# Bias table of a fused attention and expert kernel: two scalings and one hidden unit on ScalarE, sixteen transfers on GpSimd's queue

## The chip, the cores and the metric

The kernel runs on one core of a Trainium2 chip. The metric is the device time of one execution in microseconds (us), the median of three runs. The core has a matrix engine (TensorE, PE in the profile), three engines for elementwise work (VectorE is DVE, ScalarE is ACT, GpSimd is POOL) and SyncE (SP), which here only issues DMA transfers. ScalarE and GpSimd can issue transfers too.

## The reference

Attention over 8 batches, 8 heads, 576 queries and keys of 64 numbers, with a learned bias that depends on the distance of query and key, then a layer of 8 experts of which each token takes one:

```python
scores = scale * np.matmul(q, k.transpose(0, 1, 3, 2))
psi_rel = np.log1p(np.abs(rel))                       # rel = i - j
psi_i = np.log1p(np.maximum(pos[:, None], 1.0))
x = (psi_rel / psi_i)[..., None]
bias = np.maximum(x @ w1 + b1, 0.0) @ w2              # 32 hidden units, 8 heads
scores = scores + bias.transpose(2, 0, 1)[None, :, :, :]
...                                                   # softmax, times v
h = np.maximum(x[mask] @ w1[e], 0.0)                  # the expert of each token
out[mask] = gate_w[mask, None] * (h @ w2[e])
```

The bias is the same for all batches, so the kernel computes it once, ahead of the attention, as a table for 576 queries, 8 heads and 576 keys.

## The kernel before

**Stages.** First the bias table (from about 6 us to about 60 us), then attention over 32 pairs of heads (to about 555 us), then the expert layer. The order of the instructions on each engine is the order in which the Python program names them (a manual schedule). The framework adds the waits between engines.

**One block of the table.** `bias_table` (L225) goes through 32 blocks of 16 queries in the order of `SEQ`. For each block four "hidden units" of 128 rows and 576 columns are made (`bias_hidden`, L180: add a shift, then the maximum with 0). By L232 the first of the four goes to ScalarE and three to VectorE; blocks listed in `ON_DVE` have all four on VectorE. The first unit is made ahead: at each step L239 asks for those of this and the next block. TensorE multiplies each unit with the second weights (`bias_out`, L194) into a PSUM bank, of which there are three. One step later (`LAG = 1`) `bias_put` (L208) scales the bank by a number for each query, into one of eight buffers that are used in turn (`bias_outs`, L176). The scaling is ScalarE's, but VectorE's for the blocks in `PUT_DVE`.

**Where the table goes.** SP issues one transfer of 288 KB for each of the 32 blocks, to `NBm` (L218), which serves queries 0 to 511. The last 64 queries are blocks 32 to 35. They are run in the order 32, 34, 33, 35 by `bias_late` (L255), whose steps the first two units of the attention loop call (`LATE`, L133): 32 and 34 are put in the first unit, 33 and 35 in the second. Each of these blocks is written to `NBr` by four transfers of 72 KB (L223), `par` 0 and 1 times `a` 0 and 1; the two of `par` 0 on SP's queue, the two of `par` 1 on GpSimd's.

**What reads them.** Scores of a pair are made in five units (`scores`, L381): units 0 to 3 read `NBm`, unit 4 reads `NBr`. A VectorE reduction (L409) adds the scores in PSUM and the table, and takes the minimum. The reduction of unit 4 reads rows of all of `NBr`, so it needs all sixteen transfers. It also frees the PSUM bank into which TensorE makes the next pair's first scores (L395).

**What GpSimd and SP do around it.** In the order of its program GpSimd has the transfers of blocks 32 and 34, a copy of unit 0 (`compact`, L429), the transfers of 33 and 35, the copy of unit 1, the low part of pair 1's queries (`split`, L379), the copy of unit 2, the low part of its keys (L379), the copy of unit 3. SP has, behind the eight transfers of L223, the values of pair 0 (L365) and the queries and keys of pair 2 (L350 to L355).

Of the kernel before, what the change touches and what calls it, by code (L numbers as in the profile page):

```python
# [44 lines left out]
GS = 8  # L45
# [63 lines left out]
class Attn:  # L109
# [9 lines left out]


    SEQ = (0, 4, 1, 5, 2, 6, 3, 7, 8, 12, 9, 13, 10, 14, 11, 15, 16, 20, 17, 21, 18, 22, 19, 23, 24, 28, 25, 29, 26, 30, 27, 31)
    ON_DVE = (4,)


    LAG = 1
    PUT_DVE = (22, 31, 33)
    TURN0, SPLIT0, QK1 = (4, 8), (6, 10), (9, 10, 11, 12, 13, 14, 15, 16)
    V0 = (0, 1)
    ROUTE = (6, 7, 8, 15, 16, 18)
# [78 lines left out]
    def bias_put(self, blk, parts):  # L208
        nc = self.nc
        o = next(self.bias_outs)  # L210
        for cols, ps in parts:
            if blk in self.PUT_DVE:
                nc.vector.tensor_scalar_mul(o[:, cols], ps, self.rpsi[:, blk : blk + 1])
            else:
                nc.scalar.activation(o[:, cols], ps, AF.Copy, scale=self.rpsi[:, blk : blk + 1])
        if blk < NMAIN:
            c, k = divmod(blk, GS)
            nc.sync.dma_start(self.NBm[k:P:GS, H * c : H * c + H, :], o)  # L218
        else:
            for par in range(2):  # L220
                for a in range(2):
                    r = 64 * par + 2 * (blk - NMAIN) + a
                    (nc.sync, nc.gpsimd)[par].dma_start(self.NBr[r : 64 * par + 64 : GS, :, :], o[64 * a + par : 64 * a + 64 : 2, :])  # L223

    def bias_table(self, hooks):  # L225

# [3 lines left out]
        def ahead(blk, cg):  # L230
            if blk < NMAIN and (blk, cg) not in ready:
                by = "act" if cg == 0 and blk not in self.ON_DVE else "dve"  # L232
                ready[blk, cg] = self.bias_hidden(blk, cg, by)

        with self.tc.tile_pool(name="bps", bufs=3, space=PSUM) as pp:
            done = []
            for at, blk in enumerate(self.SEQ):
                ps = pp.tile([P, 1024], F32, tag="bps", name=f"bps{blk}")
                for b in self.SEQ[at : at + 2]:  # L239
                    if b not in self.ON_DVE:  # L240
                        ahead(b, 0)
# [1250 lines left out]
```

## Time and profile before

| | |
|---|---|
| median of three runs | 995.18 us (994.75 to 996.34) |
| the profiled execution | 995.04 us, its span 993.2 us |
| TensorE busy | 968.3 us, 97% of the span |
| VectorE, ScalarE, GpSimd busy | 704.7, 710.2, 319.0 us |

The profile is of one execution, in us from the start of its span. An operation is named by its line in the kernel, its engine, and the tiles it writes and reads (`out<-in`). A bracket at the end of a row of the timeline is the time that the engine was idle before it, and what ended that wait. The share of the DMA engines is a mean over 16 of them and can come out a little over 1, since packets overlap.

### The profile page before, as it was taken

The page shows a single profiled execution, that of the slowest core. Times are in us where ns is not written, and L with a number is a line of the kernel's source. Part 1 is how long each engine was busy: PE and PEld are TensorE (multiplying, and loading weights), DVE is VectorE, ACT ScalarE, POOL GpSimd, SP SyncE. Part 2 cuts the span into 40 slices and gives each one's busy share as a digit, 9 for nine tenths or more (in the row PEclk, how much of TensorE's full clock was granted, in tenths as well). Part 3 has the DMA queues.
Part 4 walks back from the last instruction along what each step waited for, and adds up shares of the span by engine and source line. Part 5 has one row for each costly group of instructions (what it writes and reads, how often), then busy time and mean ns, then how long its engine had stood idle before and what let it go on. Part 6 is the DMA issues. An engine that isn't in the chain of part 4 may idle for free.

```text
span 993.2 us, 22468 instructions
## 1 busy us (share of the span) xinstructions
PE 968.3 (97%) x8110; PEld 760.0 (77%) x8110; DVE 704.7 (71%) x1441; ACT 710.2 (72%) x1366; POOL 319.0 (32%) x497
## 2 busy tenths in 40 slices
PE   7989999999999999999999999999999999999996
PEld 4556766767667677776667699989999998989895
DVE  8976677776777777777877677986665665555555
ACT  6989888888888888888888655555545555555554
POOL 1633333635436254362542523511111111111111
PEclk9999999999999999999999999999999999999999
DMA  6997855465554656546469441221118821252510
GB/s 164 191 192 149 214 113 104 102 132 110 131 101 101 133 106 135 101 101 136 94 119 207 136 113 54 81 64 43 44 49 223 248 66 43 87 172 82 175 44 25
DMA packets 327480, 116.34 MB, mean 117 GB/s; under 512 B 283438, under 2 KB 304302, under 8 KB 327362
## 3 DMA queue, kind: packets, MB, share of 16 engines
q1 hardware_dynamic: 320914, 95.21, 43.4%
q0 software_dynamic: 6304, 19.63, 5.9%
q8 instruction: 65, 1.06, 0.5%
q14 instruction: 53, 0.43, 0.2%
q10 hardware_dynamic: 144, 0.00, 0.0%
HBM read 144.34 MB, written 33.34 MB: 179 GB/s over the span
## 4 chain that ended last, share of the span: by engine, by line
PE 78%; DVE 7%; ACT 4%; issue 3%; DMA 1%; SPq 0%; POOL 0%; DVEq 0%; POOLq 0%; ACTq 0%
PE p L1211 19%; PE p L1228 16%; PE sps L395 13%; PE xps L481 13%; PE eps L439 10%; ACT Eb L424 2%; ACT eT L327 2%; PE eps L445 1%; DVE Eb L409 1%; PE xps L467 1%; DVE xTb L329 1%; DVE w1lo L1169 1%; PE xps L753 1%; DVE w2lo L1169 1%; PE xps L784 1%
## 5 line engine op out<-in xcount | busy, mean ns | idle before, releaser
L409 DVE CUSTOM_DVE_ANT_0 Eb<-sps,NBm 128x576 f32<-128x576 f32 x256 | 183.6, 754 | 122.3 <-PE sps L395 49.0
L424 ACT ACTIVATE Eb<-Eb,mn 128x576 f32<-128x576 f32 x288 | 220.9, 769 | 10.5 <-DVE mn L409 9.5
L327 ACT ACTIVATE eT<-eps 128x512 f32<-128x512 f32 x256 | 148.9, 595 | 54.3 <-PE eps L439 53.3
L395 PE MATMUL sps<-QK 64*128 64x288 f32 (+1 forms) x1728 | 170.7, 309 | 4.1 <-DVE mn L409 3.6
L395 PEld LDWEIGHTS sps<-QK 64*128 64x128 f32 (+1 forms) x1728 | 133.4, 185 | 44.6 <-DVE mn L409 25.3
L1211 PE MATMUL p<-QK,w1hi 128*128 128x256 f32 x1136 | 160.9, 284 | 0.1
L439 PE MATMUL eps<-idf,Eb 128*128 128x128 f32 x1024 | 148.8, 279 | 3.7 <-DVE eT L329 1.9
L1211 PEld LDWEIGHTS p<-QK,w1hi 128*128 128x128 f32 x1136 | 147.2, 192 | 3.3 <-issue 1.8
L481 PE MATMUL xps<-eT,vraw 128*64 128x288 f32 x1024 | 149.3, 416 | 0.0
L439 PEld LDWEIGHTS eps<-idf,Eb 128*128 128x128 f32 x1024 | 112.6, 141 | 37.5 <-issue 13.3
L1214 DVE SCALAR_TENSOR_TENSOR hl<-p,hh 128x512 fp32r<-128x512 f32 x72 | 49.7, 691 | 119.0 <-ACT hh L1213 98.2
L1237 POOL DMA_INDIRECT out<-mo,idt x36 | 47.0, 1307 | 256.7 <-ACT mo L1236 169.4
L1213 ACT ACTIVATE hh<-p 128x512 fp32r<-128x512 f32 x72 | 43.1, 598 | 117.9 <-PE p L1211 113.7
L1228 PE MATMUL p<-w2hi,hh 128*128 128x512 f32 x288 | 112.3, 390 | 0.0
L1228 PE MATMUL p<-w2hi,hl 128*128 128x512 f32 x288 | 112.3, 390 | 0.0
L429 POOL COPY rem<-Eb 128x128 f32<-128x128 f32 x128 | 37.2, 292 | 215.9 <-ACT Eb L424 214.8
L1169 DVE TENSOR_TENSOR w2lo<-NBm,w2hi 128x1024 fp32r<-128x1024 f32 x72 | 89.5, 1243 | 16.2 <-ACT w2hi L1168 16.2
L481 PEld LDWEIGHTS xps<-eT,vraw 128*64 128x64 f32 x1024 | 62.3, 136 | 40.0 <-issue 12.6
L1211 PE MATMUL p<-QK,w1lo 128*128 128x256 f32 x568 | 91.3, 283 | 0.0
L1169 DVE TENSOR_TENSOR w1lo<-NBm,w1hi 128x1024 fp32r<-128x1024 f32 x72 | 84.1, 1208 | 0.0
L1211 PEld LDWEIGHTS p<-QK,w1lo 128*128 128x128 f32 x568 | 78.3, 192 | 0.0
L1168 ACT CAST w2hi<-NBm 128x1024 fp32r<-128x1024 f32 x72 | 74.9, 1040 | 0.0
(220 smaller groups left out, 1453.2 us busy)
## 6 DMA issues: line engine op xcount, KB each, us to landing
NBm<-moe_w SPq DMA_DIRECT2D x84, 512.0 KB
NBm<-moe_w SPq DMA_DIRECT2D x42, 1024.0 KB
NBr<-xg SPq DMA_DIRECT2D x80, 128.0 KB
kraw<-k SPq DMA_DIRECT2D x128, 72.0 KB
xd<-xt SPq DMA_DIRECT2D x128, 72.0 KB
vraw<-v SPq DMA_DIRECT2D x64, 128.0 KB
NBm<-xTb SPq DMA_DIRECT2D x24, 288.0 KB
NBm<-moe_w SPq DMA_DIRECT2D x3, 2048.0 KB
```

What stands on the lines that cost most here:

```text
L327: self.nc.scalar.activation(out, ps, AF.Copy, scale=scale)
L395: nc.tensor.matmul(self.sps[h][:, half, 0:HS], QK[o, q, qs], QK[o, k, HS * half : HS * half + HS], start=i == 0, stop=i == 2, skip_group_c ...
L409: nc.vector.tensor_tensor_reduce(out=e.rearrange("p (t w) -> p t w", t=2), in0=self.sps[h][:, :, 0:HS], in1=nb.rearrange("p (t w) -> p t w ...
L424: self.nc.scalar.activation(e, e, AF.Exp, bias=mn, scale=-1.0, accum_out=sm)
L439: nc.tensor.transpose(ps[:, k, :], e[:, part, P * k : P * k + P], self.idf)
L481: nc.tensor.matmul(ps[out : out + 64, :], lhsT, rhs, tile_position=(row, out), skip_group_check=True, **kw)
L1168: self.nc.scalar.copy(h, w)
L1169: self.nc.vector.tensor_tensor(l, w, h.bitcast(F32), op=ALU.subtract)
L1211: nc.tensor.matmul(ps[:, a, :], w[:, c, fs], x[:, c, :], start=i == 0, stop=i == len(ops) - 1)
L1214: nc.vector.scalar_tensor_tensor(hl[:, sl, :], ps, 0.0, hh[:, sl, :].bitcast(F32), op0=ALU.max, op1=ALU.subtract)
L1228: nc.tensor.matmul(ps, h[:, f, sl], m[:, f, :], start=i == 0, stop=i == len(ops) - 1)
L1237: nc.gpsimd.indirect_dma_start(out=self.out, out_offset=IndirectOffsetOnAxis(ap=ids, axis=0), in_=o, in_offset=None, bounds_check=self.n_t ...
```

## The change

`ON_DVE` becomes empty: the first hidden unit of block 4 goes to ScalarE, and is asked for one step earlier, with that of block 0. `PUT_DVE` loses blocks 22 and 31: ScalarE does these two scalings; block 33 stays with VectorE. All sixteen transfers of L223 are issued by GpSimd; before, eight were SP's.

```diff
-    ON_DVE = (4,)
+    ON_DVE = ()
...
-    PUT_DVE = (22, 31, 33)
+    PUT_DVE = (33,)
...
-                    (nc.sync, nc.gpsimd)[par].dma_start(self.NBr[r : 64 * par + 64 : GS, :, :], o[64 * a + par : 64 * a + 64 : 2, :])
+                    nc.gpsimd.dma_start(self.NBr[r : 64 * par + 64 : GS, :, :], o[64 * a + par : 64 * a + 64 : 2, :])
```

## Rows read from the trace of the kernel before

**Rows 1.** The page: the span

```profile
span 993.2 us, 22468 instructions
```

**Rows 2.** Stretches: length, busy time by engine, clock, DMA share, GB/s

```profile
55.00:60.00 5.00, 5.00 (x74) 2.95 (x68) 4.99 (x13) 4.16 (x9) 2.65 (x4) 1.00 1.05 240
65.00:70.00 5.00, 3.91 (x33) 3.28 (x33) 2.73 (x6) 5.00 (x13) 2.57 (x4) 1.00 0.77 180
70.00:75.00 5.00, 4.08 (x42) 3.54 (x44) 2.21 (x6) 3.63 (x8) 0.00 (x0) 1.00 0.75 108
75.00:100.00 25.00, 24.99 (x232) 17.47 (x230) 17.48 (x41) 22.60 (x54) 8.73 (x16) 1.00 0.74 147
```

**Rows 3.** The chain in order of time, from 65 us: start, length, what

```profile
65.15 0.59 SPq L223
...
65.78 4.33 DMA vraw<-v
...
70.92 1.07 PE sps L395 x12
```

**Rows 4.** Timeline of VectorE: start, length, operation, count, idle before

```profile
23.26 2.23 DVE L191 TENSOR_SCALAR eT<-xTb,xrb 128x576 f32<-128x576 f32 x5
...
39.21 0.82 DVE L213 TENSOR_SCALAR xTb<-bps,xrb 128x576 f32<-128x576 f32 x1
39.94 0.90 DVE L191 TENSOR_SCALAR rT<-xTb,xrb 128x576 f32<-128x576 f32 x1
...
53.27 0.82 DVE L213 TENSOR_SCALAR xt<-bps,xrb 128x576 f32<-128x576 f32 x1
...
67.97 0.69 DVE L329 COPY eT<-eps 128x512 f32<-128x512 f32 x1 [0.50 <-PE eps L439]
70.09 0.76 DVE L409 CUSTOM_DVE_ANT_0 Eb<-sps,NBr 128x576 f32<-128x576 f32 x1 [1.43 <-DMA vraw<-v]
```

**Rows 5.** Timeline of ScalarE

```profile
9.68 0.74 ACT L215 ACTIVATE xTb<-bps,xrb 128x576 f32<-128x576 f32 x1 [2.58 <-PE bps L199]
...
38.56 0.79 ACT L215 ACTIVATE xTb<-bps,xrb 128x576 f32<-128x576 f32 x1
39.18 0.83 ACT L189 ACTIVATE eT<-xTb,xrb 128x576 f32<-128x576 f32 x1
...
43.00 0.74 ACT L215 ACTIVATE xt<-bps,xrb 128x576 f32<-128x576 f32 x1 [1.03 <-PE bps L199]
...
55.61 0.69 ACT L215 ACTIVATE xTb<-eps,xrb 128x512 f32<-128x512 f32 x1 [2.14 <-PE xps L199]
```

**Rows 6.** Timeline of SP's queue

```profile
57.52 8.22 SPq L223 DMA_DIRECT2D NBr<-xTb  x8
```

**Rows 7.** Waits of SP's queue, 50 to 66 us: total, times, longest

```profile
SPq L223 <- DMA NBm<-xTb: 2.5, 4, 0.8
SPq L223 <- DMA NBm<-xt: 1.4, 2, 0.8
```

**Rows 8.** Timeline of GpSimd

```profile
56.81 2.66 POOL L223 DMA_DIRECT2D NBr<-xTb  x4 [16.29 <-ACT xTb L215]
60.54 0.29 POOL L429 COPY rem<-Eb 128x128 f32<-128x128 f32 x1 [1.07 <-ACT Eb L424]
60.77 2.14 POOL L223 DMA_DIRECT2D NBr<-xTb  x4
...
64.02 1.55 POOL L379 TENSOR_TENSOR QK<-qT,QK 128x640 fp32r<-128x640 f32 x1 [0.34 <-ACT QK L378]
...
67.36 1.42 POOL L379 TENSOR_TENSOR QK<-kT,QK 128x576 fp32r<-128x576 f32 x1 [0.77 <-ACT QK L378]
```

**Rows 9.** Line 223: GpSimd's eight, ns min/median/max, starts; its landings

```profile
L223 POOL DMA_DIRECT2D NBr<-xTb x8: 541/541/1005, 56.8 to 62.4; - x8
...
DMA to landing us min/median/max: 5.1/5.4/7.9
```

**Rows 10.** The page: a GpSimd transfer of the attention stage, us to landing

```profile
xg<-xrb,pos POOLq DMA_INDIRECT x21, 3.4
```

## Prediction

> **What bounds the kernel now.** The profiled execution took 995.04 us, of which the span is 993.2 [rows 1]; the median of the runs shown is 995.18, so what the sum adds to the span is added to that median. The first view to read is the table of stretches: from 75 us on TensorE is busy 24.99 us of 25 [rows 2]. There nothing that VectorE, ScalarE or a queue saves can shorten the run, and whatever delays TensorE's entry into that stretch is passed on whole. The change lies ahead of it, so its worth is the time at which the stretch begins. The second view is the chain of waits, which says what sets that time: the last transfer of L223 on SP at 65.15, a DMA that lasts until 70.1, VectorE's reduction L409, and at 70.92 the first scores of pair 1 [rows 3]. VectorE's timeline says the same from the waiting side: the reduction that reads `NBr` starts at 70.09 after 1.43 us idle that a DMA ended; the row names `vraw`, which this instruction does not read, so it is the transfers to `NBr` that use the same counters [rows 4]. The operation ahead of the reduction is a copy that starts at 67.97 and takes 0.69, so without the wait it could start at 68.66. That is the most that the present wait can give back. The third view is the stage itself: from 55 to 60 us VectorE is busy 4.99 us of 5, and the DMA engines are full (1.05, 240 GB/s) [rows 2]. So the bias stage has two limits, VectorE and the transfers, and a faster VectorE meets the second at once.
>
> **The unit and the two scalings.** VectorE loses one unit: five take 2.23 us, so about 0.43 each [rows 4]. It loses the scalings at 39.21 and 53.27; from the first to the next operation are 0.73 us [rows 4]. Together 0.43 + 2 x 0.73 = 1.89 us less. ScalarE gains one unit (0.83 busy) and two scalings (0.79 busy, the next operation starts 0.62 later) [rows 5], so 2.1 to 2.4 us. Its idle times cover that: the unit goes into the 2.58 us ahead of 9.68, the scaling of block 22 into the 1.03 us ahead of 43.00, that of block 31 into the 2.14 us ahead of 55.61 [rows 5]. What is left is ScalarE's earlier start: ahead of 43.00 the scaling's 0.62 takes the place of 1.03 of waiting, and VectorE's unit gives another 0.43, so the scalings from there on come about 1.03 - 0.62 + 0.43 = 0.84 us earlier. That is less than VectorE's saving up to there (0.43 + 0.73 = 1.16), because then ScalarE is the one that has no gap. I carry 0.9 us to the first transfer of L223 on GpSimd: 56.81 [rows 8] becomes 55.9. By itself it is worth nothing at the end: the table's transfers that stand ahead are bound by full DMA engines, which finish when they finish. If the cover on ScalarE fails, the 2.1 us stand in the way of block 32's scaling (a rival below).
>
> **The transfers: who waits.** SP loses eight issues, from 57.52 to 65.74, 8.22 us for issues of 0.59 [rows 3, 6]. The gaps among them are waits for transfers to `NBm`, four from `xTb` and two from `xt` [rows 7], data that L223 neither reads nor writes. Counting back eight issues on SP from the first six transfers of L223 gives just those (blocks 25, 29, 26, 30 from `xTb`, 27 and 31 from `xt`). So a queue has eight completion counters, and a transfer isn't issued before the one eight places ahead of it has landed. GpSimd's eight are the first on its queue and wait for no counter: the first four take 2.66 us, the other four 2.14 [rows 8]. With sixteen on that queue the ninth waits until the first has landed. This wait is new, and the sum hangs on it.
>
> First to eighth: 55.9 + 1.0 + 7 x 0.54 = 60.7 [rows 9]; the copy of unit 0, 0.29 [rows 8], ends at 61.0. The ninth (block 33; its data are ready by then) needs the landing of the first. The longest of GpSimd's eight took 7.9 us to land, the shortest 5.1 [rows 9]; I read the longest as the first, issued into the fullest engines, so it landed at 56.81 + 7.9 = 64.7. If its landing moves with its issue, that is 63.8; if the full engines hold it, 64.7. I take 64.3, nearer to the second half, because the share of 1.05 says that it was the engines that held it. GpSimd stands from 61.0 to 64.3, some 3.3 us. Ninth to sixteenth: seven more issues at 0.54 to 0.58 bring the start of the last to 68.2 and its end to 68.8.
>
> Then its landing and VectorE's waits, counter by counter. From SP's last issue at 65.15 to the reduction at 70.09 were 4.94 us [rows 3, 4]: the upper end. GpSimd's transfers of the attention stage land after 3.4 us in the median [rows 10]: the lower end. After 65 us the engines are at 0.77 and 0.75 [rows 2], neither full nor free; I take 4.2. The reduction starts at 68.2 + 4.2 = 72.4, against 70.09: **+2.3 us**. TensorE's next scores wait for it, and from there the delay is carried to the end: 995.18 + 2.3 = 997.5.
>
> Bounds of this case: 63.8 + 0.1 + 7 x 0.54 + 3.4 = 71.1, so +1.0; and 65.0 + 7 x 0.58 + 4.94 = 74.0, so +3.9.
>
> **What is queued behind the waiting instruction.** On GpSimd: the copy of unit 1 (0.29), the low parts of pair 1 (1.55 and 1.42), the copies of units 2 and 3 between and behind them [rows 8]. From 68.8 that gives 68.8 + 0.29 + 1.55 + 0.29 + 1.42 = 72.4 for the low part of the keys, where it was 68.8. Pair 1's scores need it about 0.3 us after they start (they start with the high parts), and by the sum they start at 72.4 + 0.83 = 73.2, so it is just covered; the cover is 1.1 us. SP's next transfers (the values of pair 0, the queries and keys of pair 2) go out up to 8 us sooner. Nobody waits for them, so they are worth nothing, and they share the engines with the sixteen: that is in the 4.2.
>
> **A rule weighed.** The trace shows GpSimd's transfer that was issued at 56.8 landing up to 7.9 us later, where 3.4 is usual later on [rows 9, 10]: it was held behind what SP had queued. The Trainium skill, "DMA: Bandwidth & Descriptors", section "Queues, rings and completion order", says that each engine takes turns between the queues that have work, packet by packet. By that rule the first transfer would not stand behind SP's backlog but land in about 3.4 us, before 60, and the ninth would find its counter free. The row speaks against the rule at this place; what it would give is the second case below.
>
> **The rivals.** (1) The forecast: ninth behind first, +2.3. (2) **The counter is free in time**, the case on the other side. It decides at 61.0, when GpSimd comes to the ninth: if the first lands by then, which is 5.1 us after 55.9, the shortest landing of rows 9, there is no stall. The sixteenth then starts at 61.0 + 7 x 0.54 = 64.8, the reduction at 64.8 + 4.2 = 69.0, just behind the copy's 68.66: -1.1, so 994.1. For it: a shorter backlog if the earlier scalings let the table's transfers start sooner. Against it: the 7.9, and engines at 1.05. (3) **GpSimd's own queue becomes the bound**: the last transfers land fast, and the low part of the keys at 72.4, where it was 68.8 and pair 1's scores read it 0.3 us after 70.92, holds TensorE. That is +1.2, so 996.4. (4) **ScalarE becomes the bound of the bias stage**: its gaps are not where the work lands, block 32's scaling comes 1 to 2 us later instead of 0.9 earlier, and all of the sum moves with it: about +3.7, so 998.9. Against it: the gap of 2.14 lies right where block 31's scaling goes.
>
> **How the numbers follow.** Forecast 0.72, (2) 0.12, (3) 0.10, (4) 0.06. The predicted time is 997.5. Within 0.2% is within 2.0 us, about what a measurement of this kernel can tell from no change, and the forecast lies just over that. In its bounds of +1.0 to +3.9 with the middle at 2.3 I give 0.63 to more than 2.0. Slower: 0.72 x 0.63 + 0.05 = 0.50. Within: 0.72 x 0.37 + 0.10 + 0.09 of case (2) = 0.45. Faster: 0.05, what is left of (2), which can't exceed 1.4 us by the reduction alone and needs the whole stage to move. The range leaves out (2) and the worst of (4) and takes in the bounds of the forecast and (3): +1.0 - 0.7 (for the spread of the runs) to +4.1, so 995.5 to 999.3.
>
> **What would show it.** In GpSimd's timeline the transfers of L223 in two groups, eight from 55.9 to 60.7 and eight from about 64.3 to 68.8, with an idle of some 3 us between, ended by a DMA to `NBr`: right. Sixteen without that gap: step two is wrong, and (2) follows. VectorE's row of L409 on `NBr` near 72.4 with a longer DMA wait than 1.43: right; if a GpSimd row releases TensorE instead, (3). ScalarE's row at 55.61 should come near 54.7, and VectorE's first reduction about 0.9 earlier than now; if they don't, the first step is wrong. And if from 75 us on TensorE shows idle that wasn't there, the delay is not carried whole and my sum is too large.

## The result, and the profile after

The changed kernel takes **1003.67 us** in the median of six runs (1002.64 to 1004.39), the kernel before 995.07 in six runs beside it (993.88 to 996.34): a ratio of 1.0089, 95% interval 1.0079 to 1.0099. It is slower by 8.6 us, where 2.3 were forecast and 4.3 was the upper end of the range. The span of the profiled execution went from 993.2 [rows 1] to 1001.8, also 8.6.

Where the time went in is shown best by one line, the first products of the weights with the values (L481), whose start says when attention has got going. The two rows are the line's answer of the kernel before and of the changed one: shortest, median and longest instruction in ns, then the first and the last start.

```profile
L481 PE MATMUL xps<-eT,vraw x1024: 406/406/458, 74.8 to 562.0; 128*64 128x288 f32 x171
```

```profile
L481 PE MATMUL xps<-eT,vraw x1024: 406/406/458, 83.3 to 570.5; 128*64 128x288 f32 x171
```

From first to last start there are 487.2 us in both: everything was lost ahead of 83.3, by 8.5 us, and from there on it is carried to the end unchanged.

GpSimd's timeline of the changed kernel, which answers to [rows 8]:

```profile
55.84 4.86 POOL L223 DMA_DIRECT2D NBr<-xTb  x8 [2.19 <-ACT xTb L215]
60.69 0.30 POOL L429 COPY rem<-Eb 128x128 f32<-128x128 f32 x1
64.15 1.17 POOL L223 DMA_DIRECT2D NBr<-xTb  x2 [3.16 <-DMA NBr<-xTb]
65.81 1.07 POOL L223 DMA_DIRECT2D NBr<-xTb  x2 [0.48 <-DMA NBr<-xTb]
67.28 0.54 POOL L223 DMA_DIRECT2D NBr<-xTb  x1 [0.40 <-issue]
68.03 1.07 POOL L223 DMA_DIRECT2D NBr<-xTb  x2 [0.21 <-issue]
69.51 0.54 POOL L223 DMA_DIRECT2D NBr<-xTb  x1 [0.41 <-DMA NBr<-xTb]
...
72.02 1.39 POOL L379 TENSOR_TENSOR QK<-kT,QK 128x576 fp32r<-128x576 f32 x1
```

Eight transfers go out at once, then the ninth waits 3.16 us for a transfer to `NBr`, and later ones wait again, in small portions. The landing times of line 223 have grown against [rows 9]:

```profile
DMA to landing us min/median/max: 6.5/7.7/9.1
```

VectorE's copy and its reduction on `NBr`, which answer to [rows 4], and TensorE's rows around them:

```profile
67.24 0.69 DVE L329 COPY eT<-eps 128x512 f32<-128x512 f32 x1 [0.51 <-PE eps L439]
77.14 0.76 DVE L409 CUSTOM_DVE_ANT_0 Eb<-sps,NBr 128x576 f32<-128x576 f32 x1 [9.21 <-DMA NBr<-xTb]
```

```profile
67.86 1.09 PE L439 MATMUL eps<-idf,Eb 128*128 128x128 f32 x8
77.96 1.81 PE L395 MATMUL sps<-QK 64*128 64x288 f32 x12 [9.01 <-DVE mn L409]
...
82.27 1.06 PE L395 MATMUL sps<-QK 64*128 64x288 f32 x12
```

The copy is done 0.7 us earlier than before, the reduction comes 7.05 us later (77.14 against 70.09), after a wait of 9.21 instead of 1.43. TensorE stands for 9.01 us, and its first scores then take 1.81 us instead of 1.07 [rows 3].

The stretches of the changed kernel (columns as in [rows 2]: length, busy time of PE, PEld, DVE, ACT and POOL, granted clock, DMA share, GB/s):

```profile
60.00:65.00 5.00, 3.70 (x34) 2.82 (x32) 4.34 (x10) 4.36 (x11) 1.76 (x5) 1.00 1.18 179
65.00:70.00 5.00, 3.19 (x27) 2.56 (x23) 2.13 (x5) 4.63 (x11) 3.50 (x7) 1.00 1.26 134
70.00:75.00 5.00, 0.00 (x0) 0.00 (x0) 0.00 (x0) 0.00 (x0) 3.64 (x6) 0.59 1.24 124
75.00:80.00 5.00, 2.04 (x14) 1.76 (x15) 0.82 (x3) 0.87 (x2) 0.00 (x0) 0.50 0.88 111
80.00:85.00 5.00, 5.00 (x46) 4.08 (x46) 2.88 (x9) 3.96 (x10) 0.40 (x2) 0.89 0.37 57
```

Two things are to be seen. From 65 to 75 us the DMA engines are full (1.26, 1.24), where they were at 0.77 and 0.75 [rows 2]. And behind the idle stretch the granted clock is 0.50, the lower of TensorE's two levels (1.2 GHz). What fills the engines stands in the timeline of SP's queue:

```profile
56.78 1.59 SPq L365 DMA_DIRECT2D vraw<-v  x2
59.20 0.62 SPq L366 DMA_DIRECT2D vrem<-v  x1
60.46 0.72 SPq L350 DMA_DIRECT2D qraw<-q  x1
...
71.49 0.43 SPq L355 DMA_DIRECT2D kraw<-k  x1
```

Without its eight issues of L223, SP starts the values of pair 0 at 56.78, where its last issue of L223 came at 65.15 before [rows 3] and the values behind that. The queries and keys of pair 2 follow from 60.46 on, 67.45 before.

So far these are readings. Theory A: the new wait exposes the later eight transfers to SP's loads, which now go out some nine us sooner, and the idle time that follows costs TensorE its clock as well. Rivals: the edits of the bias stage; the wait alone; the loads alone.

### The profile page after: what moved, and what is told of

It is laid out like the page before. It is cut to its first block, busy times and chain, and to the rows that moved or that the text cites. A ratio compares the mean times of both kernels' runs of the same rounds, so it can differ in the third digit from the quotient of the medians.

```text
span 1001.8 us, 22476 instructions
## 1 busy us (share of the span) xinstructions
PE 967.7 (97%) x8110; PEld 760.7 (76%) x8110; DVE 703.5 (70%) x1438; ACT 711.6 (71%) x1369; POOL 340.0 (34%) x505
## 4 chain that ended last, share of the span: by engine, by line
PE 80%; DVE 7%; ACT 6%; issue 3%; DMA 3%; POOL 1%; DVEq 0%; SPq 0%; POOLq 0%; ACTq 0%
PE p L1211 19%; PE p L1228 16%; PE sps L395 13%; PE xps L481 13%; PE eps L439 10%; PE bps L199 2%; ACT Eb L424 2%; DMA NBr<-xTb 2%; ACT eT L327 2%; PE eps L445 1%; PE xps L467 1%; DVE Eb L409 1%; DVE xTb L329 1%; DVE w1lo L1169 1%; PE xps L753 1%
## 5 line engine op out<-in xcount | busy, mean ns | idle before, releaser
L327 ACT ACTIVATE eT<-eps 128x512 f32<-128x512 f32 x256 | 148.8, 594 | 55.9 <-PE eps L439 55.0
L481 PE MATMUL xps<-eT,vraw 128*64 128x288 f32 x1024 | 149.3, 416 | 0.0
L481 PEld LDWEIGHTS xps<-eT,vraw 128*64 128x64 f32 x1024 | 62.3, 136 | 40.0 <-issue 12.8
L379 POOL TENSOR_TENSOR QK<-kT,QK 128x576 fp32r<-128x576 f32 x32 | 72.3, 2259 | 19.0 <-ACT QK L378 18.6
```

The costliest lines, as they stand in the source:

```text
L327: self.nc.scalar.activation(out, ps, AF.Copy, scale=scale)
L379: nc.gpsimd.tensor_tensor(lo, x, hi.bitcast(F32), op=ALU.subtract)
L481: nc.tensor.matmul(ps[out : out + 64, :], lhsT, rhs, tile_position=(row, out), skip_group_check=True, **kw)
```

## The experiments

The table holds what the profiled execution of each kernel shows, worked out from its rows: the start of the reduction on `NBr`, the time to it from GpSimd's first transfer of L223, TensorE's idle time ahead of pair 1's first scores, and the time from their start to that of the next scores. The last columns are the median of the runs and the ratio to the kernel before, run beside them, with its 95% interval. The medians of those runs of the kernel before were 995.13 (e1 to e4), 994.55 (e5 to e8), 994.41 (e9 to e12) and 994.00 (e13), and what is said to be lost in us is meant against them.

| kernel | reduction | from first transfer | TensorE idle | scores to scores | median | ratio |
|---|---|---|---|---|---|---|
| before | 70.09 | 13.3 | 1.24 | 2.92 | 995.07 | |
| changed | 77.14 | 21.3 | 9.01 | 4.31 | 1003.67 | 1.0089 (1.0079 to 1.0099) |
| e1, bias edits only | 68.13 | 12.6 | 0.31 | 2.92 | 993.79 | 0.9993 (0.9983 to 1.0002) |
| e2, transfers only | 75.18 | 18.8 | 6.74 | 4.62 | 1004.64 | 1.0104 (1.0089 to 1.0119) |
| e3, loads held | 69.72 | 13.8 | 1.77 | 3.21 | 995.30 | 1.0003 (0.9990 to 1.0015) |
| e6, values early | 70.07 | 15.3 | 3.01 | 2.92 | 998.24 | 1.0044 (1.0032 to 1.0056) |
| e11, the same again | 70.46 | 15.2 | 3.14 | 4.47 | 997.54 | 1.0033 (1.0022 to 1.0044) |
| e7, queries and keys early | 73.86 | 19.1 | 6.80 | 5.34 | 1002.54 | 1.0080 (1.0058 to 1.0102) |
| e8, other loads early | 73.90 | 19.2 | 6.83 | 4.37 | 1002.03 | 1.0078 (1.0061 to 1.0095) |
| e10, eight on ScalarE | 76.94 | 21.0 | | 2.93 | 1001.99 | 1.0073 (1.0058 to 1.0089) |
| e4, split by block | 69.64 | 13.5 | 1.48 | 2.93 | 993.91 | 0.9988 (0.9979 to 0.9997) |
| e12, the same again | 68.02 | 13.2 | 0.92 | 2.93 | 994.12 | 0.9994 (0.9985 to 1.0003) |
| e13, split, other loads early | 71.47 | 15.7 | 3.64 | 5.30 | 998.61 | 1.0048 (1.0031 to 1.0065) |
| e5, long filler | 74.51 | 19.8 | | 2.93 | 1003.45 | 1.0096 (1.0080 to 1.0113) |
| e9, short filler | 74.54 | 19.4 | 1.32 | 2.92 | 1002.10 | 1.0085 (1.0067 to 1.0103) |

The same sixteen transfers among the same loads (changed, e2, e5, e9) need 18.8 to 21.3 us to the reduction. A single profile is thus good to about 2.5 us there; where a smaller difference is used below, it says so.

**Which part of the change: e1 and e2.** e1 is the changed kernel with the old split of L223, e2 the old bias stage with all of L223 on GpSimd.

```diff
-                    nc.gpsimd.dma_start(self.NBr[...
+                    (nc.sync, nc.gpsimd)[par].dma_start(self.NBr[...
```

> The unit and the two scalings alone, the transfers split over SP and GpSimd as before. Both theories of the loss (A: the loads of pair 0 and pair 2, which SP now issues 8 us sooner, share the DMA engines with the sixteen; B: sixteen on GpSimd's queue are slow whatever runs beside them) expect no loss here: the last transfer of L223 on SP still waits for the table's transfers, so the reduction on NBr comes at 69 to 70 us, against 70.09, and the time is 0 to 1 us below that of before.

```diff
-    ON_DVE = ()
+    ON_DVE = (4,)
...
-    PUT_DVE = (33,)
+    PUT_DVE = (22, 31, 33)
```

> All sixteen transfers on GpSimd, the unit and the scalings as before. If the transfers carry the loss, the reduction on NBr comes at 77 to 78 us and the time is 8 to 9.5 us above that of before (the changed kernel: 8.6). If the bias edits had a share in it, clearly less than 8.

VectorE's row on `NBr` in e1, then in e2:

```profile
68.13 0.76 DVE L409 CUSTOM_DVE_ANT_0 Eb<-sps,NBr 128x576 f32<-128x576 f32 x1 [0.51 <-DMA vraw<-v]
```

```profile
75.18 0.76 DVE L409 CUSTOM_DVE_ANT_0 Eb<-sps,NBr 128x576 f32<-128x576 f32 x1 [6.93 <-DMA NBr<-xTb]
```

The bias edits cost nothing: the reduction comes 1.96 us earlier than in the kernel before, and the median lies 1.3 us lower, within what the interval can't tell from nothing. The transfers alone bring all of the loss, 9.5 us by the medians, though the reduction of the one profile comes earlier than the 77 to 78 expected.

**Which loads: e3, e6, e11, e7, e8.** e3 is the changed kernel, but SP's values of pair 0 can't start before a VectorE instruction ahead of the reduction on `NBr` has written two columns of their tile, and the queries and keys of pair 2 stand behind the values on SP's queue.

```diff
+    def load_v(self, n, hold=False):
...
+        if hold:
+            nc.vector.memset(t[:, :, 0, 0:1], 0.0)
...
-        tail.setdefault(self.V0, []).append(lambda: self.load_v(0))
+        tail.setdefault((0, 4), []).append(lambda: self.load_v(0, hold=True))
+        tail.setdefault((0, 4), []).append(lambda: self.load_qk(2))
...
-                        if n + 2 < n_pair:
+                        if 0 < n < n_pair - 2:
```

> The changed kernel with SP's loads held: a write of two columns of vraw by VectorE, behind the reductions of unit 3, stands ahead of the values of pair 0, and the queries and keys of pair 2 are issued behind them, so that SP issues both from about 67 us on (before: 65.78, changed: 56.78). Nothing is left out. Theory A (the early loads slow the sixteen): the ninth transfer still waits until about 64, but the last is issued near 68.3 and lands in 4 to 5 us, the reduction on NBr comes at 72 to 73.5, and the time is 2 to 3.5 us above that of before. Theory B (GpSimd's queue alone): the reduction stays at 76 to 77.5 and the time at 7.5 to 9 above.

GpSimd's rows, the landing of line 223, VectorE's row and the stretch from 60 us:

```profile
55.88 4.79 POOL L223 DMA_DIRECT2D NBr<-xTb  x8 [3.24 <-ACT xTb L215]
60.67 0.31 POOL L431 COPY rem<-Eb 128x128 f32<-128x128 f32 x1
63.39 4.27 POOL L223 DMA_DIRECT2D NBr<-xTb  x8 [2.41 <-DVE mn L411]
```

```profile
DMA to landing us min/median/max: 2.2/3.3/7.0
```

```profile
69.72 0.76 DVE L411 CUSTOM_DVE_ANT_0 Eb<-sps,NBr 128x576 f32<-128x576 f32 x1 [1.96 <-POOL rem L431]
```

```profile
60.00:65.00 5.00, 3.77 (x32) 2.88 (x32) 4.30 (x10) 4.35 (x11) 2.59 (x7) 1.00 0.53 107
```

The wait ahead of the ninth is still there: GpSimd stands from 61.0 to 63.4 (the row names VectorE, whose result had been there long; the longest landing of 7.0 puts the first transfer's at 62.9). But the later eight go out in one row, the median landing is 3.3 instead of 7.7 us, and the ratio is 1.0003. **With the loads held, the sixteen on one queue cost nothing that can be measured.** I had still expected some 2 to 3.5 us from the wait by itself, and that was too much. The loads are held a little longer here than in the kernel before: SP starts them at 67.80 instead of 65.78. What is left of the wait shows at another place, GpSimd's work behind the sixteen: the reduction's own wait is ended by GpSimd's copy (the row above), 0.1 us behind the last landing, and the low part of the keys is done late, so that TensorE's first scores take 1.35 us instead of 1.07.

e6 holds the queries and keys only (576 KB by the page's sizes of DMA issues) and leaves the values (288 KB) early; e7 does the reverse; e8 holds everything and loads 768 KB of other data, that nobody reads, in long rows at the early place.

```diff
+        tail.setdefault((0, 4), []).append(lambda: (self.nc.vector.memset(self.qraw[0][:, 0:1], 0.0), self.load_qk(2)))
...
-                        if n + 2 < n_pair:
+                        if 0 < n < n_pair - 2:
```

> The changed kernel with only the queries and keys of pair 2 held (a write of one column of their tile by VectorE behind unit 3); the values of pair 0 (288 KB in packets of 256 bytes) go out early, at 57 us. If the packets of 128 bytes of the queries and keys slow the sixteen: the reduction on NBr at 70 to 72, the time 0 to 2 us above before. If the values do it: the reduction above 74, the time 5 us or more above.

```diff
-        tail.setdefault(self.V0, []).append(lambda: self.load_v(0))
+        tail.setdefault((0, 4), []).append(lambda: self.load_v(0, hold=True))
```

> The other half: the values of pair 0 held, the queries and keys of pair 2 (12 transfers, packets of 128 bytes) early, from 57 us on. If the packets of 128 bytes do it, most of the loss is here: the reduction on NBr at 74 to 78, the time 5 to 9 us above before. If it is the sum of bytes beside the sixteen, e6 and e7 share the loss, each 2 to 5 us.

```diff
+        def early():
+            for k in range(3):
+                self.nc.sync.dma_start(self.xrb[2 + k][:, 0:512], self.io["moe_w1"][0, P * k : P * k + P, 0:512])
+        tail.setdefault((0, 1), []).append(early)
```

> All of those loads held, and in their place SP issues at the same time three loads of 256 KB in rows of 2048 bytes into buffers that are unused until later (768 KB that nobody reads). If bytes beside the sixteen are what slows them, the loss comes back: the reduction on NBr at 73 to 77, 4 to 8 us above before. If it is the small packets: the reduction at 70 to 72, 0 to 2 us above.

The landings of line 223 in e6, e7 and e8:

```profile
DMA to landing us min/median/max: 2.3/4.8/7.6
```

```profile
DMA to landing us min/median/max: 5.5/6.7/8.1
```

```profile
DMA to landing us min/median/max: 3.2/6.4/9.4
```

In the order of the bytes that go early, from none to 864 KB (0, 288, 576, 768, 864), the way from the first transfer to the reduction is 13.8, 15.3, 19.1, 19.2 and (four profiles) 18.8 to 21.3 us. Of these steps only that from 288 to 576 KB is larger than what a single profile is good for. By the medians e6 lost 3.7 us, e8 7.5 and e7 8.0, so the loss was not shared evenly by e6 and e7. The long rows of e8 do much as the short ones of the queries and keys, if with a third more bytes, so it is not the many small packets by themselves.

The way in which e8 loses is not quite that of the changed kernel. From 65 us on its engines are no longer full, and its last transfer lands after 4.8 us; but landings of up to 9.4 us among its first eight have put the issue of the last four off to 67.38:

```profile
67.38 2.14 POOL L223 DMA_DIRECT2D NBr<-xTb  x4 [1.13 <-DMA NBr<-xTb]
```

```profile
65.00:70.00 5.00, 2.89 (x22) 2.50 (x22) 1.38 (x5) 3.58 (x8) 3.71 (x8) 1.00 0.73 164
```

**Does it need the wait: e10 and e13.** e10 gives the eight transfers of blocks 33 and 35 to ScalarE.

```diff
-                    nc.gpsimd.dma_start(self.NBr[...
+                    (nc.gpsimd if blk in (32, 34) else nc.scalar).dma_start(self.NBr[...
```

> The changed kernel with the eight transfers of blocks 33 and 35 issued by ScalarE, so that no queue has a ninth transfer behind a first, while SP's loads stay as early as in the changed kernel. Theory A (the loss needs both: loads beside the sixteen, and a later transfer that waits for an earlier one's landing): the last transfer issued by 65 to 67 instead of 69.5, reduction of unit 4 at 71 to 74; time +1 to +5. Rival B (the bytes beside the sixteen are the whole loss, the wait adds nothing): reduction at 76 to 78 as in the changed kernel, +8. Rival C (the wait is the whole loss, the crowd costs nothing): reduction at or before 70.1, within 0.2% of before. ScalarE's eight issues at some 0.5 us may push its own work; its timeline tells how far.

It doesn't tell, for it did two other things. The first row is from the waits of SP's queue (total, times, longest), the others from ScalarE's timeline:

```profile
SPq L897 <- DMA NBr<-xTb: 8.9, 1, 8.9
```

```profile
59.50 3.73 ACTq L223 DMA_DIRECT2D NBr<-xTb  x4
...
64.26 4.21 ACTq L223 DMA_DIRECT2D NBr<-xTb  x4
68.52 0.77 ACT L424 ACTIVATE Eb<-Eb,mn 128x576 f32<-128x576 f32 x1 [4.29 <-DMA NBr<-xTb]
```

A small transfer on SP's queue waited 8.9 us for one that ScalarE had issued (in the trace both count on the same semaphore), so SP's loads came late (from 68.5) and not early; and ScalarE's issues waited for landings too and held up its exponentials by 4.29 us. The time is that of ScalarE's work. Inconclusive on the question.

e13 asks it in another way: the split by block, e4, in which SP issues blocks 33 and 35 and GpSimd has no ninth transfer, and ahead of SP's eight the three loads of e8.

```diff
-                    nc.gpsimd.dma_start(self.NBr[...
+                    (nc.gpsimd if blk in (32, 34) else nc.sync).dma_start(self.NBr[...
```

> The changed kernel with the sixteen split by block: GpSimd issues the eight of blocks 32 and 34, SP the eight of 33 and 35. So GpSimd's ninth, and its wait for the landing of the first, are gone, and SP's loads stand behind its eight as before. Both theories expect the loss to go: the reduction on NBr at 69 to 70.5 us, the time within 1 us of that of before. If it stays above 3 us, neither the wait for the first landing nor the loads is the cause.

> The split by block (GpSimd issues blocks 32 and 34, SP blocks 33 and 35) once more with more runs, since its first interval ended just below 1 (0.9979 to 0.9997). If the gain of VectorE's 1.9 us is real but limited by the reduction's floor of 68.66 against 70.09, the ratio is 0.9985 to 0.9995; if it was chance, 1.000.

```diff
+        def early():
+            for k in range(3):
+                self.nc.sync.dma_start(self.xrb[2 + k][:, 0:512], self.io["moe_w1"][0, P * k : P * k + P, 0:512])
+        tail.setdefault((0, 1), []).append(early)
         for u, k in self.LATE:
```

> The split by block, in which no queue has a ninth of the sixteen behind a first, with the three 256 KB loads of e8_long_rows (unread) issued by SP at the same early place, ahead of its eight transfers of blocks 33 and 35; the values, queries and keys stay late as in the split. With sixteen on GpSimd's queue the same three loads brought the reduction of unit 4 to 73.9. Theory A (the loss needs the loads and the wait of a later transfer for an earlier one's landing): SP's eight go out by 66 as without the loads, the reduction comes at 69.5 to 71.5, time +0 to +1.5. Rival B (the bytes beside the sixteen are enough): reduction at 73 to 75, TensorE idle some 6 us, granted clock below 1 after it, time +5 to +7. In between: SP's own eight counters make its sixth to eighth transfer of the block wait for the three loads; its waits then name xrb or xrk.

VectorE's row of e13, and two rows of the waits of SP's queue:

```profile
71.47 0.76 DVE L409 CUSTOM_DVE_ANT_0 Eb<-sps,NBr 128x576 f32<-128x576 f32 x1 [3.83 <-DMA qraw<-q]
```

```profile
SPq L223 <- DMA xrk<-moe_w: 1.2, 1, 1.2
...
SPq L223 <- DMA xrb<-moe_w: 0.6, 1, 0.6
```

From first transfer to reduction the same three loads add 2.2 to 2.5 us to the split (13.2 and 13.5 to 15.7, no more than what a single profile is good for) and 5.3 to the sixteen on one queue (13.8 to 19.2). In the split, too, there is a wait: SP's eighth transfer goes out at 66.9 and not by 66, and SP's waits for these loads, 1.8 us in all, are among the causes. The reduction fell into theory A's span, at its upper edge; the time, 4.6 us above the kernel before, lies between theory A's 0 to 1.5 and rival B's 5 to 7. Of it, 2.4 us are TensorE's clock: the next scores follow after 5.30 us instead of 2.92.

So the loads are needed: without them the loss is gone (e3). They also cost 4.6 us where the sixteen are split. With the same loads, one queue for all sixteen costs more than the split (7.5 against 4.6 us by the medians, 19.2 against 15.7 from first transfer to reduction). How the wait adds to it can be read from the rows: a late landing among the first eight delays the issue of the transfer eight places on. **That the loss needs both is not shown**: without loads the two kinds differ by 0.0009 to 0.0015 in the ratio (e3 against e12 and e4), with them by 0.0030, and the intervals don't tell these apart.

The split by block itself ended below 1 in one set of runs (0.9988) and not clearly in the other (0.9994). A gain of 0.1% is possible and not settled; it has no ninth transfer on GpSimd's queue and SP's loads stay late, and its reduction, at 68.02 and 69.64, comes close behind VectorE's copy.

**What the idle time costs: e5, e9, and e11 beside e6.** e5 and e9 put 48 and 26 products, that nobody reads, ahead of pair 1's first scores.

```diff
+                if (n, u) == (1, 0):
+                    ps = self.xbank()
+                    self.xbank()
+                    for _ in range(48):
+                        self.nc.tensor.matmul(ps[:, 0:P], self.idf, self.idf, start=True, stop=True)
```

> The changed kernel with 48 products of the identity with itself on TensorE behind unit 4 of pair 0, into a bank that nobody reads; they fill most of TensorE's wait for the reduction on NBr, and nothing is left out. Theory: of the 8.6 us, 7.05 are the later reduction and about 1.5 are TensorE's clock, granted at its lower level from about 72 to 82 us after the idle. Then the reduction stays at 77 us, the clock stays at 1.00, and the time is 6.5 to 7.5 us above that of before. Rival: the clock costs nothing, since other waits cover it: 8 to 9 above.

> The changed kernel with 26 extra matrix products of 128x128 (nobody reads them) ahead of pair 1's first scores, instead of the 48 that ran 10.72 us and outlasted the wait. At 0.223 us a product they take 5.8 us and end near 73.7, before the reduction of unit 4. Theory A (about 1.5 us of the loss is TensorE's clock, granted at its lower level after some 9 us idle): granted clock 0.9 to 1.00 in 70 to 80 us instead of 0.59 and 0.50, first scores of pair 1 at 1.0 to 1.1 us instead of 1.81, reduction at 74.5 to 77, and from its scores to the next unit's about 2.9 us instead of 4.4; time 1001.5 to 1002.5. Rival (the clock costs nothing because later work catches up): time as the changed kernel, 1003.2 to 1004.2, with the same reduction.

In e5 the filler outlasted the wait (it ended at about 78.5, the reduction began at 74.51), so its time says nothing. TensorE's rows, a stretch and the row of L481 of e9 (each of the 26 products stands as two in the first row):

```profile
68.08 5.97 PE L570 MATMUL xps<-idf 128*128 128x128 f32 x52
75.36 1.06 PE L395 MATMUL sps<-QK 64*128 64x288 f32 x12 [1.32 <-DVE mn L409]
...
78.28 1.06 PE L395 MATMUL sps<-QK 64*128 64x288 f32 x12
```

```profile
75.00:80.00 5.00, 4.64 (x46) 3.85 (x48) 2.24 (x7) 3.83 (x9) 0.31 (x2) 1.00 0.58 93
```

```profile
L481 PE MATMUL xps<-eT,vraw x1024: 405/406/458, 79.3 to 566.3; 128*64 128x288 f32 x171
```

The clock stays at 1.00, and the next scores follow after 2.92 us as in the kernel before, instead of 4.31: the clock's part is 1.4 us in this profile. L481 starts 4.0 us sooner than in the changed kernel: 1.4 of the clock, and 2.6 of a reduction that came sooner in this profile. The runs don't show the gain: e9 lies 7.7 us above the kernel before beside it, the changed kernel 8.6, and the intervals of the two ratios overlap. They also hold what comes behind L481, and that is not the same in all profiles: from its last start to the end of the span are 431.2 us before, 431.3 in the changed kernel and 433.0 in e9, between 430.7 (e13) and 433.2 (e2) in the others. So the rows carry the 1.4 us, and the times neither show nor exclude it.

e11 repeats e6, whose runs lay between 995.9 and 1001.2.

> The kernel that holds the queries and keys of pair 2 back but loads the values of pair 0 early, once more, since its runs lay between 995.9 and 1001.2 while the profile is of the quickest. If the spread is the landing of the last transfers, which decides between a short and a long idle time of TensorE, the median is again 997 to 999.5, and a profile of a slower run shows the reduction later than 70.1 and a granted clock under 1 in 70 to 80 us. If it was a matter of that chip, the runs lie within 1.5 us of each other.

They lay between 996.7 and 1000.4 this time. TensorE's first scores and the stretch from 70 us, in e6 and then in e11:

```profile
70.90 1.06 PE L395 MATMUL sps<-QK 64*128 64x288 f32 x12 [3.01 <-DVE mn L409]
```

```profile
71.28 1.41 PE L395 MATMUL sps<-QK 64*128 64x288 f32 x12 [3.14 <-DVE mn L409]
```

```profile
70.00:75.00 5.00, 4.10 (x42) 3.55 (x44) 2.21 (x6) 3.29 (x8) 1.10 (x2) 1.00 0.65 119
```

```profile
70.00:75.00 5.00, 3.72 (x23) 3.44 (x24) 2.21 (x6) 2.10 (x5) 1.56 (x2) 0.68 0.73 131
```

The two wait for nearly the same time, 3.01 and 3.14 us, but in the one the clock stays at 1.00 and in the other the stretch has 0.68; the next scores follow after 2.92 and 4.47 us. Their spans, 994.1 and 996.5, differ by 2.4, of which 0.38 is the later start. A part of the spread of these runs can so be the clock. The mean granted clock of every run is on record: in e6 it is 0.997 in the quickest and 0.993 in the slowest run, but 0.995 both at 996.35 and at 1000.14 us, so the clock is not all of it.

## Why the prediction was wrong

The direction and the mechanism held, the size did not. Step by step:

- **The bias edits** were right. GpSimd's first transfer starts at 55.84 (55.9 forecast), VectorE's first reduction 0.74 us earlier (57.32 against 58.06; 0.9 forecast), ScalarE's scaling at 54.63 (54.7). ScalarE's gap covered the work, so rival (4) didn't come about, and e1 prices the part at nothing or a small gain. Rival (4) was priced too low in any case: 1 to 2 us later instead of 0.9 earlier is 1.9 to 2.9, on top of 2.3, and not +3.7.
- **The ninth behind the first** was right to 0.15 us: 64.15 for 64.3, after 3.16 us (3.3). Some of that is luck. The first transfer landed after 7.8 us, at 63.6, so its landing moved with its issue (the 63.8 of the prediction) and was not held at 64.7; and between that landing and the ninth's start went 0.5 us that the sum didn't have. Rival (2), the counter free in time, didn't occur, and with it the result that the rule weighed would have given here: that the DMA engines take turns between the queues (the Trainium skill, "DMA: Bandwidth & Descriptors", section "Queues, rings and completion order") did not bring the first transfer down before 61.0.
- **Ninth to sixteenth** failed first: I issued them at 0.54 to 0.58 us each, 3.9 in all, as if only the ninth had to wait. They took 5.4, with waits of 0.2 to 0.5 for the landings of the ones eight places ahead: the fifth landed at 66.7 and the thirteenth went out at 67.28, the eighth at 69.2 and the sixteenth at 69.51. The last starts at 69.51 instead of 68.2: **1.3 us**.
- **The landing of the last** is the step that failed most: 4.2 us forecast between bounds of 3.4 and 4.94, **7.6** measured (69.51 to 77.14), so **3.4 us**. I had seen that SP's loads go out up to 8 us sooner, and wrote them off: "they are worth nothing, and they share the engines with the sixteen: that is in the 4.2". But the upper bound came from a stretch at 0.77 of the engines [rows 2], in which SP's loads came only behind the last of its eight (65.78 against 65.15), and the lower from transfers of the attention stage [rows 10]. With the loads moved ahead, 65 to 75 us runs at 1.26 and 1.24, and the row for full engines was among mine: 5.1 to 7.9 us [rows 9], issued into a stretch at 1.05 [rows 2]. e3 shows it: with the loads held, the median landing is 3.3 and the last transfer lands after 2.4 us.
- **Carried whole** was almost right, and lacked a term: from 77.14 on, TensorE lost another **1.4 us** to the granted clock, which was 1.00 throughout in the rows that I read.

The sum: 2.3 + 1.3 + 3.4 + 1.4 = 8.4, against 8.6 measured.

- **Rival (3)**, the low part of the keys as the bound, was hidden behind the late reduction here: it ended at 72.02 + 1.39 = 73.4 (72.4 forecast), before the first scores at 77.96. Where the loads are held (e3) it shows, and costs 0.3 us.

What the Trainium skill says in "DMA: Bandwidth & Descriptors", section "Issuing engines are not separate DMA queues", bears on the step that failed: transfers begun by ScalarE, SP or GpSimd "will ultimately run on the same 16 DMA engines and interleave with each other". The runs agree, with 7.7 us to landing beside SP's loads and 3.3 without them.

## What to carry to other kernels

When transfers move off a queue, look at what stands behind them there: it now starts earlier, and into the very stretch in which the moved transfers have to land, so price their landing by rows of engines as full as they will be, not as they were. A queue on which a transfer waits for the landing of the one eight places ahead turns each late landing into a late issue; this kernel lost nothing measurable to that wait without the loads, 4.6 us to 768 KB of loads where the transfers were split over two queues, and 7.5 to 8.6 us where sixteen on one queue met the loads. If the new wait leaves TensorE idle for some us, look at the granted clock behind it: where it fell, the next scores came 1.4 to 2.4 us later on top.

## What the runs showed of the hardware that I had not expected

- **In this program SP's and ScalarE's transfers wait for each other.** In e10 SP's small transfer of L897 stood 8.9 us for a transfer to `NBr` that ScalarE had issued, since the program counts both on one semaphore. GpSimd's queue showed no such tie: its sixteen transfers in the changed kernel count on eight semaphores of their own. Whether the chip would ask for this sharing is not shown.
- **What an idle time costs in clock did not grow with its length here.** After 3.14, 3.64, 6.74, 6.80, 6.83 and 9.01 us (e11, e13, e2, e7, e8, changed) the next scores followed 1.4 to 2.4 us later than at full clock (4.31 to 5.34 instead of 2.92), with no order by the idle time. After 3.01 us (e6) the clock stayed at 1.00.
- **The loads take their time from whoever waits.** 864 KB that went out sooner moved the landing of other transfers from a median of 3.3 (e3) to 7.7 us (changed).
